# More load places for the raw queries, keys and values, and GpSimd as a third engine for SBUF passes and for the softmax division

## The chip, the cores and the metric

The kernel runs on one core of a Trainium2 chip. The metric is device time in microseconds (us), first to last instruction plus launch and end. The core has five instruction streams that run side by side and wait for each other through semaphores: TensorE (PE, matmuls; its weight loads are a row of their own, PEld), VectorE (DVE), ScalarE (ACT), GpSimd (POOL) and SyncE (SP), which here issues nearly all DMAs. Each takes its instructions strictly in the order of its own queue. GpSimd reads and writes SBUF only, not PSUM.

## The reference

Inputs are float64. Attention with 8 global keys and a local window of 96 keys, then a two-layer ELU network over the same rows:

```python
scores = 1/sqrt(D) * q @ k.T                    # B=4, H=8, S=768, D=64
keep   = (pos_k < 8) | (0 <= pos_q - pos_k < 96)
scores = where(keep, scores - slope[h] * dist, -1e9)
a      = exp(scores - max);  a = a / (sum(a) + 1e-9)
x      = (a @ v), heads side by side            # 3072 x 512
h      = x @ w_in                               # 512 -> 2048
g      = where(h > 0, h, exp(min(h, 0)) - 1)
out    = g @ w_out                              # 2048 -> 512, float32
```

## The kernel before

**Work.** The 3072 rows are 12 groups of 256 (two tiles of 128). For a group the attention of 8 heads (four head pairs) gives x, kept as a rounded half `xh` and a rest `xl`; then 16 chunks `fc` of the hidden layer follow: 12 matmuls into `h` (line 623: xh with both halves of w_in, xl with one), an ELU over ScalarE and VectorE into `e` (629 to 631), its rounded half `gh` (ScalarE, 632) and rest `gl` (VectorE or GpSimd, 633), and 6 matmuls into `o` (645). Weights come as float64 bits; `weight` (360) turns each 128x512 piece into fp32 by one ScalarE and four VectorE passes (374 may go to GpSimd), rounds it into the upper half of `w` (381) and subtracts for the lower half (393, VectorE).

**Attention.** Groups 0 to 3 use `heads32`: queries are scaled in place (420), scores, softmax, a division of `pr` by the row sum (`norm`, 497, from 533; ScalarE or VectorE), a PE transpose into `t`, a copy into `pt`, and the product with the values into `pv`. Groups 4 to 11 use `head`: the same softmax, the division (578, VectorE only), a 32x32 transpose on VectorE (584), and a trip through DRAM (`dd`) that turns the blocks into `ph`.

**Order.** Nothing is ordered by hand. Every step is an `Op` with a due time, and for each engine that may take it a cost in ns and a flag that says whether it occupies the port that the planner lets VectorE and GpSimd share. `Plan.order` (102) is a greedy list scheduler: it picks the engine and the next step by these costs, due times and free buffers ("slots"), and so fixes each engine's queue. What runs is this queue, whatever the steps really last. `SLOTS` and `EARLY` (730 to 750) say which SBUF places a class of tile may use: raw queries and values are `rqv`, raw keys `rk`. In the first groups they lie in places of weights 12 to 15 and of other tiles that are not in use yet. A load is issued on SP's queue once its place is free, and loads of weights from chunk 2 on stand behind the loads of the heads that the builder had listed by then (714).

**Start.** Until the first `h` matmul the run writes fill matmuls (`none<-fill`, 806) wherever the planner's PE would idle over 300 ns, one per 240 ns of it.

Of the kernel before, what the change touches and what calls it, by code (L numbers as in the profile page):

```python
# [12 lines left out]
ALU = mybir.AluOpType  # L13
# [3 lines left out]
P = 128  # L17
# [3 lines left out]
W = NT * P  # L21
BIG = float(2 ** 100)

HI, LO = 0, 1
# [181 lines left out]
def act(n, psum=False, extra=0.0):  # L206
    return (("ACT", (55 if psum else 97) + 0.834 * n + extra, False),)


def dve(n, fast=False, port=False):  # L210
    return (("DVE", (75 + 0.521 * n) if fast else (70 + 1.042 * n), fast or port),)


def pool(n, two=True):
    return (("POOL", (30 + 2.58 * n) if two else (50 + 1.1 * n), True),)
# [25 lines left out]
class Kernel:  # L241
# [118 lines left out]
    def weight(self, which, fc, due, after):  # L360
        nc, p, DM = self.nc, self.plan, self.DM
        tag = f"w{which}{fc}"
        bits = self.sb(tag, "bits", [P, 2 * DM], I32)
        g = self.sb("io", "g", [P, DM], I32)
        w = self.sb(tag, f"w{which}", [P, 2, DM], F32R)
        src = (self.w_in, self.w_out)[which][fc].bitcast(I32)
        words = lambda: bits.t.rearrange("p (n w) -> p n w", w=2)
        low, high = lambda: words()[:, :, 0], lambda: words()[:, :, 1]
        gf = lambda: g.t.bitcast(F32)
        p.add(sp(), lambda e: nc.sync.dma_start(bits.t, src), writes=[bits], due=due - 9000, after=after, nbytes=P * DM * 8)  # L370

        p.add((("ACT", 575.0, False),), lambda e: nc.scalar.activation(gf(), high().bitcast(F32), AF.Abs), [bits], [g], due - 6000)  # L372
        p.add(dve(DM, True) + (("POOL", 640.0, True),),
              lambda e: self.on(e).tensor_scalar(gf(), gf(), F64_MAX, F64_MIN, ALU.min, ALU.max), [g], [g], due - 5500)  # L374
        p.add(dve(DM, True), lambda e: nc.vector.tensor_scalar(g.t, g.t, 3, 0x3FFFFFFF, ALU.logical_shift_left, ALU.bitwise_and),
              [g], [g], due - 5000)
        p.add(dve(DM, port=True), lambda e: nc.vector.scalar_tensor_tensor(g.t, high(), -0x40000000, g.t, ALU.bitwise_and, ALU.bitwise_or),  # L377
              [bits, g], [g], due - 4500)
        p.add(dve(DM, port=True), lambda e: nc.vector.scalar_tensor_tensor(g.t, low(), 29, g.t, ALU.logical_shift_right, ALU.bitwise_or),
              [bits, g], [g], due - 4000)  # L380
        p.add(act(DM), lambda e: self.copy(e, w.t[:, HI], gf()), [g], [w], due - 3000)
        if (which, fc) in self.ON_PE:

            lw = self.bank("lw", "lw", [P, DM], ["h0", "h1"])

            def lower(e):
                nc.tensor.matmul(lw.t, self.ident.t, gf(), start=True, stop=False)
                nc.tensor.matmul(lw.t, self.minus1.t, w.t[:, HI], start=False, stop=True)

            p.add((("PE", 1500.0, False),), lower, [g, w], [lw], due - 2500)  # L390
            p.add(act(DM, True), lambda e: self.copy(e, w.t[:, LO], lw.t), [lw], [w], due - 2000)
        else:
            p.add(dve(DM, port=True), lambda e: self.minus(e, w.t[:, LO], gf(), w.t[:, HI]),
                  [g, w], [w], due - 2000)
        return w


    def pair(self, b, gi, hp, xh, xl, due, step, X):
        nc, p = self.nc, self.plan
# [4 lines left out]
        rows = X.get("rows")  # L404
        rep = 1 if rows else 2
        nq, nk = rep * W, rep * KW
        rqv = self.sb("rqv", "rqv", [P, nq + VC], slots=X.get("rqv"))
        rk = self.sb("rk", "rk", [P, nk], slots=X.get("rk"))
# [3 lines left out]
        q32 = lambda: rqv.t[:, :nq].rearrange("p (j w) -> p j w", j=rep)  # L412
        v32 = lambda: rqv.t[:, nq:].rearrange("p (t j d) -> p t j d", t=2 * NT, j=2)
        k32 = lambda: rk.t.rearrange("p (j w) -> p j w", j=rep)
        if rows:

            if "pr" in X:
                self.loads += loads
            sc = self.scale.t[:, hp:hp + 1]
            p.add(act(W) + dve(W, True), lambda e: self.scaled(e, q32()[:, 0], q32()[:, 0], sc), [rqv], [rqv], due - 9000)  # L420
            pv = self.bank("pv", "pv", [P, NT, P], X.get("pv"))
            for tiles in (range(NT),) if X.get("whole") else ((i,) for i in range(NT)):
                self.heads32(b, hp, t0, tiles, q32, k32, v32, rqv, rk, pv, due - 2 * step, 2 * step, X)
            pvs = lambda: pv.t.rearrange("p i w -> p (i w)")
            p.add(act(W, True) + dve(W), lambda e: self.copy(e, xh.t[:, hp], pvs()), [pv], [xh], due + 700)
            p.add(dve(W), lambda e: self.minus(e, xl.t[:, hp], pvs(), xh.t[:, hp]), [pv, xh], [xl], due + 800)
            if "pr" in X:
                self.held += [o for v in (rqv, rk) for o in v.readers]
            return
# [5 lines left out]
        for j in range(2):  # L435
            sc = self.q_scale(2 * hp + j)
# [3 lines left out]
        for j in range(2):  # L440
            sc = self.q_scale(2 * hp + j)
# [12 lines left out]
        x = self.sb("x", "x", [P, W])  # L454
        head = [slice(0, 64), slice(64, 128)]
        for j in range(2):
# [3 lines left out]
            r, o, d = head[j], head[1 - j], due + (NT * j - NT) * step  # L460
# [8 lines left out]
    def scaled(self, e, out, x, sc):  # L469
        if e == "ACT":  # L470
            self.nc.scalar.activation(out, x, AF.Copy, scale=sc)
        else:
            self.nc.vector.tensor_scalar(out, x, sc, None, ALU.mult)  # L473

# [13 lines left out]
    def inverse(self, st, due, slack=0.0):  # L488
# [5 lines left out]

        self.plan.add((("DVE", 290.0, False),), inverse, [st], [st], due, slack=slack)

    def norm(self, pr, lo, st, i, due, both):
        n = 2 * P - lo
        return self.plan.add((act(n, extra=90) if both else ()) + (("DVE", 130 + 0.53 * n, True),), lambda e: self.scaled(
            e, pr.t[:, lo:], pr.t[:, lo:], st.t[:, 2, i:i + 1]), [pr, st], [pr], due)  # L500

    def heads32(self, b, hp, t0, tiles, q32, k32, v32, rqv, rk, pv, due, step, X):
# [50 lines left out]
    def head(self, b, h, t0, j, qd, ql, ks, vd, pv, due, step):  # L553

        nc, p, slack = self.nc, self.plan, self.SLACK
        st = self.sb("st", "st", [P, 3, NT])
# [18 lines left out]
        for i, pr in enumerate(prs):  # L575
            d = base + i * step
            lo = 0 if t0 + i else P
            self.norm(pr, lo, st, i, d - 3000, False)

            def turn(e, i=i, pr=pr, lo=lo):  # L580
                nc.vector.transpose(tr.t[:, :, lo // P:, i].rearrange("p b a r -> p a b r"),  # L581
                                    pr.t[:, lo:].rearrange("p (a b r) -> p a b r", b=4, r=32))

            p.add(dve(2 * P - lo), turn, [pr], [tr], d - 2500)
        if not t0:
            p.add((("DVE", 200.0, False),), lambda e: nc.vector.memset(tr.t[:, :, 0, 0], 0.0), [], [tr], base - 2600)
        flat = lambda x: x.rearrange("p b a i r -> p (b a i r)")
# [23 lines left out]
    def moe(self, rows, xh, xl, f0, f1, dues, step, part, X, last):  # L611
# [4 lines left out]
        def up(fc, d):  # L616
            w1 = ws[0][fc]
            h = self.bank("h", "h", [P, W])
            for n in range(3):
                def mm1(e, n=n, h=h, w1=w1):  # L620
                    s, x = ((HI, xh), (LO, xh), (HI, xl))[n]
                    for cc in range(self.NCC):
                        nc.tensor.matmul(h.t, w1.t[:, s, cc * P:(cc + 1) * P], x.t[:, cc],  # L623
                                         start=n == 0 and cc == 0, stop=n == 2 and cc == self.NCC - 1)
                p.add(pe(self.NCC * W), mm1, [w1, xl if n == 2 else xh], [h], d + n)
            ex = self.sb("e", "e", [P, W])
            gh, gl = self.sb("gh", "gh", [P, W], F32R), self.sb("gl", "gl", [P, W], F32R)

            p.add(act(W, True), lambda e: nc.scalar.activation(ex.t, h.t, AF.Relu, scale=-1.0), [h], [ex], d - 8000)  # L629
            p.add(act(W), lambda e: nc.scalar.activation(ex.t, ex.t, AF.Exp, scale=-1.0), [ex], [ex], d - 8000)  # L630
            p.add(dve(W), lambda e: nc.vector.scalar_tensor_tensor(ex.t, ex.t, -1.0, h.t, ALU.add, ALU.max), [h, ex], [ex], d - 8000)  # L631
            p.add(act(W), lambda e: self.copy(e, gh.t, ex.t), [ex], [gh], d - 8000)
            p.add(dve(W, port=True) + pool(W) if X or last else (("POOL", 787.0, True),), lambda e: self.minus(e, gl.t, ex.t, gh.t), [ex, gh], [gl], d - 8000)
            G[fc] = gh, gl

# [46 lines left out]
    def build(self):  # L682
# [41 lines left out]
        for _, f in sorted(todo, key=lambda x: x[0]):  # L724
# [4 lines left out]

    LATE = 12  # L730
    ON_PE = []
    FIRST = {"rqv": ["rqv0", "w015", "w115"], "rk": ["rk0", "w014", "w114"], "pr": ["pr0", "pr1", "pr2", "w013", "w113"],
             "pt": ["pt0", "pt1", "w012", "w112"], "rows": True}
    EARLY = [dict(FIRST, rqv=FIRST["rqv"] + ["part0", "part1"], rk=FIRST["rk"] + ["qd0", "ql0"], pr=FIRST["pr"] + ["ks0"],
                  pt=FIRST["pt"] + ["vd0"], t=["t0", "h0"], s=["s0", "s1", "o0", "o1"], pv=["v0"]), dict(FIRST, whole=True), dict(FIRST, whole=True),
             {"rqv": ["rqv0", "ks0"], "rk": ["rk0", "qd0", "ql0"], "rows": True, "whole": True}, {}]

    SLACK, LATER = 600.0, 1200.0

# [286 lines left out]
```

## Time and profile before

| what | value |
|---|---|
| time, median of 3 runs (range) | 690.71 us (689.43 to 692.09) |
| the profiled execution | 689.4 us, span 687.6 us |
| PE, DVE, ACT, POOL busy | 667.9, 556.6, 498.3, 222.1 us |
| share of the span | 97%, 81%, 72%, 32% |
| HBM | 73.01 MB read, 23.07 MB written |

Busy PE is not PE at its peak: a matmul's end is modelled, so gaps shorter than its pipeline don't show, and fill matmuls count as busy. The idle time before a group of instructions and its releaser, and the table by stretches, tell more than the share of the span.

### The profile page before, as it was taken

The numbers are of one execution on the slowest core, as the hardware profiler recorded it, in microseconds if no ns is written. First come the engines' busy times: TensorE is split into PE (matmuls) and PEld (weight loads), VectorE is DVE, ScalarE is ACT, GpSimd is POOL, SyncE is SP. The second block draws the span as 40 slices with busy tenths as digits, with TensorE's granted clock in tenths as the row PEclk, the third lists the DMA queues.
The fourth block names the chain that finished last, engine by engine and source line by source line (L and its number), as shares of the span: only waits on it lengthen the run. The fifth ranks groups of instructions, "written<-read, shape, count | busy, mean of one in ns | idle before, by whom it ended". The sixth has DMA issues, their size and how long they took to land.

```text
span 687.6 us, 13611 instructions
## 1 busy us (share of the span) xinstructions
PE 667.9 (97%) x4461; PEld 590.4 (86%) x4461; DVE 556.6 (81%) x1647; ACT 498.3 (72%) x1400; POOL 222.1 (32%) x277
## 2 busy tenths in 40 slices
PE   9989999999999998999999999999999999999996
PEld 6768788888888987989989989989999989889895
DVE  6999999997649999978978998987888997983322
ACT  6998897885657777867867777867967867775443
POOL 1110222120014453452454463353364445233000
PEclk9999999999999999999999999999999999999999
DMA  8543980010136547455453553643652653520000
GB/s 319 194 116 114 412 340 24 1 48 1 55 122 218 163 147 210 139 171 161 154 182 111 183 153 124 209 157 103 229 164 88 228 158 107 178 93 1 32 1 33
DMA packets 65259, 97.01 MB, mean 141 GB/s; under 512 B 4640, under 2 KB 39712, under 8 KB 65184
## 3 DMA queue, kind: packets, MB, share of 16 engines
q1 hardware_dynamic: 64896, 95.96, 42.2%
q8 instruction: 36, 0.59, 0.4%
q14 instruction: 39, 0.32, 0.1%
q10 hardware_dynamic: 288, 0.13, 0.1%
HBM read 73.01 MB, written 23.07 MB: 140 GB/s over the span
## 4 chain that ended last, share of the span: by engine, by line
PE 60%; DVE 21%; ACT 7%; issue 6%; DMA 5%; POOL 1%; SPq 0%; DVEq 0%; POOLq 0%; ACTq 0%
PE h L623 26%; PE o L645 26%; DVE pr L473 3%; PE pv L604 3%; DVE tr L581 3%; ACT pr L485 2%; DVE pr L483 2%; PE s L570 2%; DVE e L631 2%; DVE x L464 2%; DVE ph L300 2%; DMA bits<-in_w_out_dram 1%; DVE ks L300 1%; DVE g L377 1%; DMA ph<-dd 1%
## 5 line engine op out<-in xcount | busy, mean ns | idle before, releaser
L623 PEld LDWEIGHTS h<-xh,w 128*128 128x128 f32 x1536 | 230.7, 189 | 30.3 <-ACT xh L292 1.4
L645 PE MATMUL o<-w,gh 128*128 128x512 f32 x768 | 242.7, 399 | 4.8 <-ACT gh L292 2.5
L623 PE MATMUL h<-xh,w 128*128 128x256 f32 x1536 | 243.4, 282 | 1.8 <-ACT xh L292 1.2
L300 POOL TENSOR_TENSOR gl<-e,gh 128x256 fp32r<-128x256 f32 x135 | 109.6, 812 | 287.2 <-ACT gh L292 251.6
L645 PEld LDWEIGHTS o<-w,gh 128*128 128x128 f32 x768 | 124.4, 188 | 20.4 <-ACT gh L292 8.8
L631 DVE SCALAR_TENSOR_TENSOR e<-e,h 128x256 f32<-128x256 f32 x192 | 79.7, 415 | 61.8 <-ACT e L630 58.3
L645 PE MATMUL o<-w,gl 128*128 128x512 f32 x384 | 128.1, 396 | 0.0
L623 PE MATMUL h<-xl,w 128*128 128x256 f32 x768 | 121.7, 280 | 0.0
L292 ACT CAST gh<-e 128x256 fp32r<-128x256 f32 x192 | 77.5, 404 | 59.5 <-DVE e L631 58.2
L629 ACT ACTIVATE e<-h 128x256 f32<-128x256 f32 x192 | 72.7, 379 | 58.8 <-PE h L623 54.9
L485 ACT ACTIVATE pr<-pr,nmax 128x256 f32<-128x256 f32 (+1 forms) x192 | 93.5, 487 | 21.5 <-DVE nmax L483 20.3
L623 PEld LDWEIGHTS h<-xl,w 128*128 128x128 f32 x768 | 104.0, 188 | 0.3 <-issue 0.2
L630 ACT ACTIVATE e<-e 128x256 f32<-128x256 f32 x192 | 79.8, 416 | 3.8
L483 DVE CUSTOM_DVE_ANT_0 pr<-s,tab 128x256 f32<-128x256 f32 (+1 forms) x192 | 72.5, 389 | 10.9 <-PE s L570 8.9
L473 DVE TENSOR_SCALAR pr<-pr,st 128x256 f32<-128x256 f32 (+1 forms) x159 | 65.6, 436 | 0.6
L645 PEld LDWEIGHTS o<-w,gl 128*128 128x128 f32 x384 | 62.3, 189 | 2.9 <-issue 0.5
L464 DVE TENSOR_TENSOR x<-pv,x 64x256 f32<-64x256 f32 x128 | 53.1, 415 | 9.2 <-ACT x L292 6.7
L581 DVE STREAM_TRANSPOSE tr<-pr 128x256 f32<-128x256 f32 (+1 forms) x128 | 52.6, 417 | 0.4
L374 POOL TENSOR_SCALAR g<-g 128x512 f32<-128x512 f32 x24 | 22.8, 955 | 91.6 <-ACT g L372 86.9
L300 DVE TENSOR_TENSOR ph<-ph 128x512 fp32r<-128x512 f32 x62 | 46.1, 744 | 2.3 <-ACT ph L292 2.0
L300 POOL TENSOR_TENSOR vd<-rqv,vd 128x512 fp32r<-128x512 f32 (+1 forms) x32 | 40.2, 1255 | 1.7
L292 ACT CAST ph<-ph 128x512 fp32r<-128x512 f32 x64 | 39.1, 611 | 1.8 <-DMA ph<-dd 1.7
(93 smaller groups left out, 844.6 us busy)
## 6 DMA issues: line engine op xcount, KB each, us to landing
rqv<-in_qkv_dram SPq DMA_DIRECT2D x32, 512.0 KB, 4.1
dd<-tr SPq DMA_DIRECT2D x64, 256.0 KB, 2.5
ph<-dd SPq DMA_DIRECT2D x64, 256.0 KB, 3.0
rk<-in_qkv_dram SPq DMA_DIRECT2D x32, 400.0 KB, 4.0
bits<-in_w_in_dram SPq DMA_DIRECT2D x16, 512.0 KB, 8.9
bits<-in_w_out_dram SPq DMA_DIRECT2D x16, 512.0 KB, 9.9
rqv<-in_qkv_dram SPq DMA_DIRECT2D x16, 384.0 KB, 3.7
out_dram<-ob SPq DMA_DIRECT2D x23, 256.0 KB, 3.7
```

Source lines behind the costliest of these rows:

```text
L292: self.nc.scalar.copy(out, x)
L300: self.on(e).tensor_tensor(out, x, y, ALU.subtract)
L464: p.add(dve(W), lambda e, r=r, s=s, xt=xt, pv=pv: nc.vector.tensor_tensor(xt(), pv.t[r, :, s], xt(), ALU.add), [pv, x], [x], d + 600 + s)
L473: self.nc.vector.tensor_scalar(out, x, sc, None, ALU.mult)
L483: p.add((("DVE", 158 + 1.042 * n, False),), lambda e: nc.vector.tensor_tensor_reduce(pr.t[:, lo:], s.t[:, m, lo:], tab, -(2.0 ** -(h + 1)) ...
L485: p.add(act(n, extra=200), lambda e: nc.scalar.activation(pr.t[:, lo:], pr.t[:, lo:], AF.Exp, bias=nm, scale=-1.0, accum_out=st.t[:, 0, i: ...
L581: nc.vector.transpose(tr.t[:, :, lo // P:, i].rearrange("p b a r -> p a b r"), pr.t[:, lo:].rearrange("p (a b r) -> p a b r", b=4, r=32))
L623: nc.tensor.matmul(h.t, w1.t[:, s, cc * P:(cc + 1) * P], x.t[:, cc], start=n == 0 and cc == 0, stop=n == 2 and cc == self.NCC - 1)
L629: p.add(act(W, True), lambda e: nc.scalar.activation(ex.t, h.t, AF.Relu, scale=-1.0), [h], [ex], d - 8000)
L630: p.add(act(W), lambda e: nc.scalar.activation(ex.t, ex.t, AF.Exp, scale=-1.0), [ex], [ex], d - 8000)
L631: p.add(dve(W), lambda e: nc.vector.scalar_tensor_tensor(ex.t, ex.t, -1.0, h.t, ALU.add, ALU.max), [h, ex], [ex], d - 8000)
L645: nc.tensor.matmul(acc[i].t, g.t[:, i * P:(i + 1) * P], w2.t[:, s], start=fc == f0 and n == 0 and s == HI, stop=fc == f1 - 1 and n == 1)
```

## The change

Three more places for `rqv` in groups 0 to 3 (the `ph` buffers, free until group 4) and two more for `rk` in groups 1 and 2 are listed in `FIRST` and `EARLY`; the lower weight half goes to GpSimd alone, and GpSimd may take the upper half, the scaling of the queries, the division of the first groups, and `gh` of the first three groups. The division of groups 4 to 11 goes to GpSimd alone. The planner's cost of the 32x32 transpose rises and gets a slack.

```diff
-        p.add(act(DM), lambda e: self.copy(e, w.t[:, HI], gf()), [g], [w], due - 3000)
+        p.add(act(DM) + pool(DM, False), lambda e: self.copy(e, w.t[:, HI], gf()), [g], [w], due - 3000)
...
-            p.add(dve(DM, port=True), lambda e: self.minus(e, w.t[:, LO], gf(), w.t[:, HI]),
+            p.add(pool(DM), lambda e: self.minus(e, w.t[:, LO], gf(), w.t[:, HI]),
...
-            p.add(act(W) + dve(W, True), lambda e: self.scaled(e, q32()[:, 0], q32()[:, 0], sc), [rqv], [rqv], due - 9000)
+            p.add(act(W) + dve(W, True) + (("POOL", 60 + 1.1 * W, True),), lambda e: self.scaled(e, q32()[:, 0], q32()[:, 0], sc), [rqv], [rqv], due - 9000)
...
+        elif e == "POOL":
+            self.nc.gpsimd.tensor_scalar(out, x, sc, 1.0, ALU.mult, ALU.mult)
...
+    def divide(self, pr, lo, st, i, due):
+        n = 2 * P - lo
+        self.plan.add((("POOL", 60 + 1.1 * n, True),), lambda e: self.nc.gpsimd.tensor_scalar(
+            pr.t[:, lo:], pr.t[:, lo:], st.t[:, 2, i:i + 1], 1.0, ALU.mult, ALU.mult), [pr, st], [pr], due)
...
-        return self.plan.add((act(n, extra=90) if both else ()) + (("DVE", 130 + 0.53 * n, True),), lambda e: self.scaled(
+        return self.plan.add((act(n, extra=90) if both else ()) + (("DVE", 130 + 0.53 * n, True), ("POOL", 60 + 1.1 * n, True)), lambda e: self.scaled(
...
-            self.norm(pr, lo, st, i, d - 3000, False)
+            self.divide(pr, lo, st, i, d - 3000)
...
-            p.add(dve(2 * P - lo), turn, [pr], [tr], d - 2500)
+            p.add((("DVE", 150 + 1.042 * (2 * P - lo), False),), turn, [pr], [tr], d - 2500, slack=300.0)
...
-            p.add(act(W), lambda e: self.copy(e, gh.t, ex.t), [ex], [gh], d - 8000)
+            p.add(act(W) + (pool(W, False) if X else ()), lambda e: self.copy(e, gh.t, ex.t), [ex], [gh], d - 8000)
...
-    FIRST = {"rqv": ["rqv0", "w015", "w115"], "rk": ["rk0", "w014", "w114"], "pr": ["pr0", "pr1", "pr2", "w013", "w113"],
+    FIRST = {"rqv": ["rqv0", "w015", "w115", "ph0", "ph1", "ph2"], "rk": ["rk0", "w014", "w114", "qd0", "ql0"], "pr": ["pr0", "pr1", "pr2", "w013", "w113"],
...
-             {"rqv": ["rqv0", "ks0"], "rk": ["rk0", "qd0", "ql0"], "rows": True, "whole": True}, {}]
+             {"rqv": ["rqv0", "ks0", "ph0", "ph1", "ph2"], "rk": ["rk0", "qd0", "ql0"], "rows": True, "whole": True}, {}]
```

Over the whole program the division of `pr` moves from 159 VectorE and 33 ScalarE instructions to 18, 25 and 149 on GpSimd; the lower weight half from 32 on VectorE to 32 on GpSimd; the scaling of queries from 7 VectorE and 9 ScalarE to 1, 8 and 7 on GpSimd; 12 `gh` and 6 upper weight halves go from ScalarE to GpSimd; of the 32 clamps of `weight` (374) GpSimd had 24 and has 26.

SP's queue before, from the load of the fifth pair's keys on (`rqv` and `rk` are loads of a head pair, `bits` a weight; a tile's number grows with its place in the plan):

```order
L411 DMA rk_159<-in_qkv_dram 128x400
L370 DMA bits_162<-in_w_in_dram 128x1024
L370 DMA bits_164<-in_w_out_dram 128x1024
L370 DMA bits_166<-in_w_out_dram 128x1024
L370 DMA bits_194<-in_w_in_dram 128x1024
L370 DMA bits_205<-in_w_in_dram 128x1024
L370 DMA bits_213<-in_w_out_dram 128x1024
L370 DMA bits_221<-in_w_out_dram 128x1024
L411 DMA rk_283<-in_qkv_dram 128x400
L411 DMA rk_356<-in_qkv_dram 128x400
```

The same place now:

```order
L411 DMA rk_159<-in_qkv_dram 128x400
L410 DMA rqv_161<-in_qkv_dram 128x768
L410 DMA rqv_163<-in_qkv_dram 128x768
L370 DMA bits_165<-in_w_in_dram 128x1024
L410 DMA rqv_173<-in_qkv_dram 128x768
L370 DMA bits_179<-in_w_out_dram 128x1024
L370 DMA bits_183<-in_w_out_dram 128x1024
L411 DMA rk_191<-in_qkv_dram 128x400
L370 DMA bits_202<-in_w_in_dram 128x1024
L370 DMA bits_213<-in_w_in_dram 128x1024
```

Three loads of queries and values of the second group have moved ahead of the first weights. Further on in the same queue, the last loads of the third group and the weights of chunk 4 behind them stood so before:

```order
L410 DMA rqv_787<-in_qkv_dram 128x768
L410 DMA rqv_824<-in_qkv_dram 128x768
L410 DMA rqv_998<-in_qkv_dram 128x768
L410 DMA rqv_1006<-in_qkv_dram 128x768
L370 DMA bits_1045<-in_w_in_dram 128x1024
L370 DMA bits_1051<-in_w_in_dram 128x1024
```

and now:

```order
L410 DMA rqv_598<-in_qkv_dram 128x768
L411 DMA rk_660<-in_qkv_dram 128x400
L410 DMA rqv_685<-in_qkv_dram 128x768
L410 DMA rqv_690<-in_qkv_dram 128x768
L370 DMA bits_729<-in_w_in_dram 128x1024
L370 DMA bits_735<-in_w_in_dram 128x1024
```

The same loads and weights have moved from tile number 1045 to 729 of the plan. On PE, the last rows ahead of the first `h` matmul of group 0 (`pv` a product with values, `t` transposes, `s` scores) were before:

```order
L522 MATMUL pv_364<-pt_391,rqv_147 64x128 x4
L806 MATMUL none<-fill 128x512 x6
L522 MATMUL pv_444<-pt_407,rqv_153 64x128 x2
L540 MATMUL t_447<-ident,pr_360 128x128 x2
L540 MATMUL t_447<-ident,pr_389 128x128 x2
L806 MATMUL none<-fill 128x512 x5
L516 MATMUL s_470<-rk_283,rqv_426 128x256
L516 MATMUL s_471<-rk_283,rqv_426 128x256
```

and now:

```order
L523 MATMUL s_407<-rk_159,rqv_157 128x256
L523 MATMUL s_408<-rk_159,rqv_157 128x256
L813 MATMUL none<-fill 128x512
L529 MATMUL pv_433<-pt_395,rqv_153 64x128 x2
L813 MATMUL none<-fill 128x512 x3
L547 MATMUL t_450<-ident,pr_378 128x128 x2
L547 MATMUL t_450<-ident,pr_393 128x128 x2
L813 MATMUL none<-fill 128x512 x3
L523 MATMUL s_468<-rk_191,rqv_161 128x256
```

Seven fills stand where eleven stood; over the whole start it is 33 instead of 43, with the same attention work ahead of the first `h`. In a late group, VectorE's rows between a row sum's inverse (`st`) and the transposes were before:

```order
L493 RECIPROCAL st_8590<-st_8590 128x2
L631 SCALAR_TENSOR_TENSOR e_8621<-e_8621,h_8568 128x256
L473 TENSOR_SCALAR pr_8566<-pr_8566,st_8590 128x256
L473 TENSOR_SCALAR pr_8603<-pr_8603,st_8590 128x256
L581 STREAM_TRANSPOSE tr_8650<-pr_8566 128x2x4x32
```

Now GpSimd's queue has the two divisions of that head, between the rest `gl` of one chunk and of the next:

```order
L300 TENSOR_TENSOR gl_8592<-e_8542,gh_8582 128x256
L501 TENSOR_SCALAR pr_8556<-pr_8556,st_8571 128x256
L501 TENSOR_SCALAR pr_8588<-pr_8588,st_8571 128x256
L300 TENSOR_TENSOR gl_8651<-e_8615,gh_8639 128x256
```

The transposes on VectorE stay behind them across engines, with other VectorE work in between.

## Rows read from the trace of the kernel before

**Rows 1.** Busy time by stretches of the span: the stretch, its length, then busy us and (x instructions) of PE, PEld, DVE, ACT and POOL, the granted PE clock, the DMA share and GB/s.

```profile
0.00:30.00 30.00, 28.50 (x170) 19.42 (x171) 24.05 (x116) 22.72 (x73) 4.84 (x23) 1.00 0.72 275
30.00:80.00 50.00, 45.81 (x374) 36.82 (x373) 46.23 (x165) 44.39 (x140) 6.20 (x9) 1.00 0.53 182
80.00:200.00 120.00, 119.75 (x802) 104.69 (x801) 101.18 (x249) 85.28 (x226) 21.36 (x20) 1.00 0.26 97
200.00:620.00 420.00, 411.96 (x2730) 374.06 (x2729) 365.30 (x1066) 316.99 (x894) 183.92 (x217) 1.00 0.50 159
620.00:687.60 67.60, 61.88 (x394) 55.42 (x392) 19.79 (x53) 28.90 (x72) 5.78 (x9) 0.99 0.05 17
```

**Rows 2.** What PE waited for in the whole span: us in total, times, longest us.

```profile
PE o L645 <- ACT gh L292: 2.5, 5, 1.0
PE t L540 <- DVE pt L294: 1.6, 1, 1.6
...
PE s L516 <- ACT rqv L471: 1.3, 1, 1.3
PE h L623 <- ACT xh L292: 1.2, 1, 1.2
```

**Rows 3.** PE's instructions in order of time in the start: start us, us, what, how many.

```profile
8.32 0.50 PE L806 MATMUL none<-fill 128*128 128x512 f32 x1
...
23.85 1.65 PE L806 MATMUL none<-fill 128*128 128x512 f32 x6
...
29.61 1.68 PE L623 MATMUL h<-xh,w 128*128 128x256 f32 x12
...
37.66 0.66 PE L540 MATMUL t<-ident,pr 128*128 128x128 f32 x4 [1.55 <-DVE pt L294]
39.57 1.14 PE L516 MATMUL s<-rk,rqv 64*128 64x256 f32 x8 [1.25 <-ACT rqv L471]
```

**Rows 4.** The fill matmuls as one group in the first 40 us: count, busy us, mean ns, idle before.

```profile
L806 PE MATMUL none<-fill 128*128 128x512 f32 x43 | 15.6, 492 | 1.4 <-POOL fill L324 1.4
```

**Rows 5.** SP's queue in order of time: start us, us from first to last issue, what.

```profile
35.60 0.33 SPq L410 DMA_DIRECT2D rqv<-in_qkv_dram  x1
...
41.77 0.33 SPq L410 DMA_DIRECT2D rqv<-in_qkv_dram  x1
...
48.91 15.62 SPq L410 DMA_DIRECT2D rqv<-in_qkv_dram  x4
64.59 0.90 SPq L370 DMA_DIRECT2D bits<-in_w_in_dram  x2
```

**Rows 6.** Pieces of the chain that ended last, between 30 and 80 us: start us, us, what.

```profile
35.60 3.39 DMA rqv<-in_qkv_dram
...
41.77 3.59 DMA rqv<-in_qkv_dram
...
65.53 9.16 DMA bits<-in_w_out_dram
```

**Rows 7.** VectorE groups of the whole span by shape: count, busy us, mean ns, idle before.

```profile
L473 DVE TENSOR_SCALAR pr<-pr,st 128x256 f32<-128x256 f32 x133 | 57.9, 455 | 0.4
...
L492 DVE TENSOR_SCALAR st<-st 128x2 f32<-128x2 f32 x96 | 24.0, 250 | 6.5 <-ACT pr L485 6.0
...
L300 DVE TENSOR_TENSOR w<-g,w 128x512 fp32r<-128x512 f32 x32 | 21.8, 682 | 0.2
...
L473 DVE TENSOR_SCALAR pr<-pr,st 128x128 f32<-128x128 f32 x26 | 8.6, 339 | 0.1
```

**Rows 8.** The same groups between 30 and 80 us alone.

```profile
L300 DVE TENSOR_TENSOR w<-g,w 128x512 fp32r<-128x512 f32 x8 | 5.5, 682 | 0.1
L473 DVE TENSOR_SCALAR pr<-pr,st 128x256 f32<-128x256 f32 x15 | 5.1, 357 | 0.0
...
L492 DVE TENSOR_SCALAR st<-st 128x2 f32<-128x2 f32 x14 | 2.3, 164 | 0.4 <-ACT pr L485 0.3
...
L473 DVE TENSOR_SCALAR rqv<-rqv,scale 128x256 f32<-128x256 f32 x5 | 1.7, 348 | 0.4 <-DMA rqv<-in_qkv_dram 0.4
```

**Rows 9.** GpSimd groups by shape: first the whole span, then the first 30 us, then 30 to 200 us, then 200 to 620 us.

```profile
L300 POOL TENSOR_TENSOR vd<-rqv,vd 128x512 fp32r<-128x512 f32 x24 | 32.0, 1333 | 1.1
...
L294 POOL CAST vd<-rqv 128x384 fp32r<-128x384 f32 x8 | 4.1, 512 | 2.7 <-PE pv L604 2.6
...
L374 POOL TENSOR_SCALAR g<-g 128x512 f32<-128x512 f32 x4 | 2.4, 626 | 13.0 <-ACT g L372 13.0
...
L374 POOL TENSOR_SCALAR g<-g 128x512 f32<-128x512 f32 x20 | 20.4, 1020 | 78.6 <-ACT g L372 73.9 <-DVE w L300 4.7
...
L300 POOL TENSOR_TENSOR gl<-e,gh 128x256 fp32r<-128x256 f32 x122 | 99.9, 819 | 203.4 <-ACT gh L292 179.3 <-PE o L645 10.1 <-PE h L623 9.3
```

More of the change, by code (lines that the diff above doesn't have):

```diff
@@ L731 @@
     ON_PE = []
-    FIRST = {"rqv": ["rqv0", "w015", "w115"], "rk": ["rk0", "w014", "w114"], "pr": ["pr0", "pr1", "pr2", "w013", "w113"],
+    FIRST = {"rqv": ["rqv0", "w015", "w115", "ph0", "ph1", "ph2"], "rk": ["rk0", "w014", "w114", "qd0", "ql0"], "pr": ["pr0", "pr1", "pr2", "w013", "w113"],
              "pt": ["pt0", "pt1", "w012", "w112"], "rows": True}
-    EARLY = [dict(FIRST, rqv=FIRST["rqv"] + ["part0", "part1"], rk=FIRST["rk"] + ["qd0", "ql0"], pr=FIRST["pr"] + ["ks0"],
+    EARLY = [dict(FIRST, rqv=FIRST["rqv"] + ["part0", "part1"], pr=FIRST["pr"] + ["ks0"],
                   pt=FIRST["pt"] + ["vd0"], t=["t0", "h0"], s=["s0", "s1", "o0", "o1"], pv=["v0"]), dict(FIRST, whole=True), dict(FIRST, whole=True),
-             {"rqv": ["rqv0", "ks0"], "rk": ["rk0", "qd0", "ql0"], "rows": True, "whole": True}, {}]
+             {"rqv": ["rqv0", "ks0", "ph0", "ph1", "ph2"], "rk": ["rk0", "qd0", "ql0"], "rows": True, "whole": True}, {}]
     SLACK, LATER = 600.0, 1200.0
```

## The prediction

> **What bounds the kernel now.** I read the table by stretches first, then what PE waited for, then PE's and SP's rows in order of time in the start, then the groups by shape. The reader is to see in the table [rows 1] that PE is the bound nearly everywhere: from 80 to 200 us it is idle for 120.00 - 119.75 = 0.25 us, from 200 to 620 us for 420 - 411.96 = 8.0 us. The granted clock is 1.00 in both, the upper level of 2.4 GHz, so it has no part in this. The change adds or takes no matmul of the computation; all it can do is shorten or lengthen the time in which PE has nothing useful to do. That time is 4.2 us from 30 to 80 us (50 - 45.81), 8.0 us later, the 43 fills of the start [rows 4], and little else: the idle time of the last stretch is mostly the end, after PE's last matmul. So some 22 us is the most that can be won, and the question is how much of each piece goes.
>
> In the early stretch the other engines are nearly full: VectorE 46.23 and ScalarE 44.39 of 50 us, GpSimd 6.20. And the chain that ended last runs there through loads [rows 6]: 3.39 and 3.59 us for two loads of queries and values, 9.16 us for a weight. SP's rows [rows 5] show why they are late: the loads of the second and third group go out one by one, six us apart, since three places make each wait for an earlier pair to be used up; four more take until 64.5, and only then, at 64.59, does the weight of chunk 4 leave. SP is idle in between.
>
> **The change part by part, start to 30 us.** Ahead of the first `h`, at 29.61 us [rows 3], stand 33 fills in place of 43, with the same attention work: by the planner's costs PE waits 10 x 240 ns less. A single fill shows 0.50 us and six in a row 1.65, so one costs (1.65 - 0.50) / 5 = 0.23 us; by mean busy time [rows 4] it would be 0.49. I take 10 x 0.23 = 2.3 us won; the ends are 4.9 won, and 1 us lost if GpSimd's passes come late and PE stands idle where the fills were. What pays for it is that some scalings and divisions of the first pairs leave VectorE and ScalarE for GpSimd.
>
> **30 to 80 us.** With six places instead of three, the loads at 35.60 and 41.77 [rows 5] go out while the first pairs are worked on. The two stalls behind them, 1.55 and 1.25 us on PE [rows 2, 3], lose their cause: scaled queries and copies that came late because a load did or VectorE was full. VectorE is also relieved: 8 lower weight halves (5.5 us), most of 15 divisions (5.1) and of 5 scalings (1.7) [rows 8], about 10 of its 46 us. GpSimd takes 8 x 1.33 us for the halves [rows 9] and some 16 divisions and scalings. A division of 128x256 on GpSimd is not in the trace; the nearest rows are its 128x512 one-input pass with 626 ns, half of which is 0.31 us, and a 128x384 copy with 512 ns [rows 9]. I take 0.37 us, nearer the first since it is the same operation. That makes 6.2 + 10.6 + 5.9 = 22.7 of 50 us on GpSimd: room enough. What is late next are the transposes' copies on two engines that are still 70% to 90% full, so of 4.2 us idle I take 3.0 as won; the ends are all 4.2, and 1 us lost.
>
> The weights: the last loads of the third group need a place that a pair three pairs earlier gives up, so chunk 4 leaves about when four pairs of the second group are done, some 15 to 20 us before 64.59. This takes the 9.16 us off the chain, but PE waited only briefly for it, and that is within the 3.0.
>
> **80 to 200 us.** 24 lower halves (24 x 0.682 = 16.4 us [rows 7]) go from VectorE to GpSimd, where they last 24 x 1.33 = 32 us. PE has 0.25 us idle, so a relief of VectorE is worth nothing here: 0, with a loss of up to 12 us if GpSimd can't keep up (first rival).
>
> **200 to 620 us.** Eight groups with 16 divisions each: 112 of 128x256 and 16 of 128x128 leave VectorE, 112 x 0.455 + 16 x 0.339 = 56 us [rows 7], and GpSimd gets 128 x 0.37 = 47 us (40 to 66 by the two ends). VectorE falls from 365 of 420 us (87%) to 309 (74%), GpSimd rises from 184 (44%) to 231 (55%) [rows 1]. The hop to another engine and back lies between the inverse and the transposes; other VectorE steps are put there in the new order. PE's 8.0 us idle here is scattered over short waits for `gh` and `xh` [rows 2], both made of ScalarE and VectorE steps that queue behind attention work. A quarter of VectorE's queue is gone in front of them, and the planner now counts the transpose near what it lasts. I take 3.0 of the 8.0 us as won; ends 8.0 won and 12 lost (second rival).
>
> VectorE's and GpSimd's passes hold each other up, and the trace has the size: the inverse's first step, 128x2, lasts 164 ns where GpSimd is 12% busy [rows 8, 1] and 250 in the mean [rows 7]; GpSimd's clamp lasts 626 ns in the first 30 us and 1020 from 30 to 200 us, where VectorE is full [rows 9]. With GpSimd's share up by a quarter, 96 inverses lose perhaps a quarter of 86 ns more, 2 us in all on an engine that gives up 56, so I book nothing.
> The Trainium skill ("SBUF — State Buffer", Who interferes with whom) makes this a lock: a VectorE operation in a two-port mode or with two SBUF inputs, or a GpSimd operation, holds the shared port pair for the whole instruction, and the other blocks. The stretched rows agree with it; by it the move wins less than its 56 us of VectorE, because a division on GpSimd holds the pair too. It also speaks against the lower halves, as "GPSIMD Engine Reference" (Engine selection) does, which puts two-input passes at about twice VectorE's time; the trace agrees with 1333 against 682 ns.
>
> **Sum.** -2.3 - 3.0 + 0 - 3.0 = -8.3 us on the profiled execution's 689.4: 681.1. Its time lies 1.3 us under the median of the runs, so against 690.71 I forecast 682.4 us (-1.2%).
>
> **The rivals.** First, on the other side: GpSimd becomes the bound of the weight stage. A chunk is used by three groups, 3 x 18 matmuls; at 61.88 us for 394 instructions [rows 1] that is 54 x 0.157 = 8.5 us a chunk. GpSimd's share of it: two lower halves, two clamps (26 of 32 clamps are its), up to two `gl` and a cast or two. Undisturbed: 2 x 1.33 + 2 x 0.63 + 2 x 0.82 + 0.7 = 6.3 us. Stretched like the clamp (1020 / 626 = 1.63): 2.2 x 2 + 1.0 x 2 + 1.6 + 1.2 = 9.2, beyond 8.5: it decides from a stretch of about 1.5 on all of its passes. Then each of 12 chunks comes about 1 us late, +12 us, less 5.3 won before: 697. For it: the clamp's rows. Against: VectorE's own port work falls by a third there, GpSimd had only 21 us of 120 to do [rows 1], and weights leave earlier and have a lead.
>
> Second: the division holds up the late groups. GpSimd takes its queue in order; `gl` waits there 203.4 / 122 = 1.7 us each for `gh` [rows 9], and a division behind it waits too, then the transposes on VectorE, the trip through DRAM, and at a group's end PE for `xh`. If all eight group ends pay 1.7 us, it is +13, less the 1.2 that one shows already [rows 2] and less 5.3: +6.7 us, 697. Against: only one such wait is in the trace at all, so the chains have a lead.
>
> Third: little changes. The fills' 2.3 us come, but stalls between 30 and 80 us only change their releaser, from loads to full VectorE and ScalarE, and the short waits later stay, being the greedy order's own: 688.4. For it: 92% and 89% busy there. Nor need the change do what it says about division: where the planner finds VectorE cheaper, `norm` stays; but 149 of 192 are on GpSimd.
>
> **How the numbers follow.** The forecast has 62% (its own range 675 to 687), little change 20%, each of the two slower cases 9%. About 0.5% (3.5 us) is what a measurement of this kernel can tell from no change: from 687.3 to 694.2. Faster: the 62 and 2 of the third case, 64%; no difference: the rest of the third and 2 of the slower ones, 20%; slower 16%. The range: the won ends add up to 4.9 + 4.2 + 8.0 = 17 us, 674; upward it takes in the third case and half-sized losses, to 694, and leaves most of the two slower cases out.
>
> **What would show it.** In the new profile: the first `h` near 27 us; loads of queries no longer six us apart, chunk 4's weight leaving before 52 us; PE idle under 2 us from 30 to 80 us; VectorE near 74% and GpSimd near 55% from 200 to 620 us with PE idle about 5 us there; a division on GpSimd of about 0.37 us, 0.6 at most. Wrong would be: PE idle of several us between 80 and 200 us with `w` or `gl` of GpSimd as releaser (first rival), or waits for `xh` at every group's end (second).

## The result, and the profile after

The changed kernel takes 674.22 us (673.97 to 675.37 over 6 runs), the kernel before 691.4 us on the same chip; the ratio is 0.9757 with a 95% interval from 0.9733 to 0.9780. That is 16.8 us less (0.0243 x 691.4), where 8.3 were forecast. The time lies 0.2 us above the low end of the range.

The table by stretches of the changed kernel, with the columns of [rows 1]:

```profile
0.00:30.00 30.00, 28.28 (x172) 19.15 (x173) 23.75 (x112) 22.30 (x76) 13.32 (x38) 1.00 0.90 343
30.00:80.00 50.00, 47.42 (x370) 37.07 (x369) 48.44 (x150) 44.32 (x134) 25.99 (x34) 1.00 0.72 263
80.00:200.00 120.00, 120.00 (x810) 106.00 (x810) 99.58 (x240) 80.75 (x211) 55.96 (x59) 1.00 0.15 53
200.00:620.00 420.00, 419.99 (x2814) 385.13 (x2813) 328.01 (x943) 322.64 (x902) 250.75 (x347) 1.00 0.50 157
```

Read the instruction counts beside the busy time. From 200 to 620 us PE is idle for 0.01 us instead of 8.0, but it issues 2814 instructions instead of 2730. An instruction of the tail takes 61.88 / 394 = 0.157 us [rows 1], so 84 more (59 of them `h`, 25 `o`) are 13.2 us of work: 5 us more than the idle time shows. From 80 to 200 us 8 more (1.3 us). Up to 80 us there are 172 + 370 - 33 fills = 509 against 170 + 374 - 43 = 501, another 1.3 us, though matmuls of several kinds are mixed there. Together 15.7 us, about the gain (the two profiled executions lie 15.2 us apart), and more than four fifths of it is in the late groups.

What PE still waited for, in the whole span:

```profile
PE s L523 <- DVE nmax L485: 1.4, 2, 1.2
PE none L813 <- POOL fill L324: 1.4, 1, 1.4
PE h L630 <- DVE e L638: 0.6, 1, 0.6
PE o L652 <- POOL w L300: 0.4, 1, 0.4
```

Four rows are left, and `xh` and `gh` of [rows 2] are gone from them. GpSimd's new passes, and the first step of the inverse on VectorE:

```profile
L501 POOL TENSOR_SCALAR pr<-pr,st 128x256 f32<-128x256 f32 x112 | 60.8, 552 | 30.2 <-DVE st L495 17.4 <-ACT gh L292 6.3 <-ACT xh L292 2.9
L300 POOL TENSOR_TENSOR w<-g,w 128x512 fp32r<-128x512 f32 x32 | 43.5, 1366 | 25.6 <-ACT w L292 25.3
...
L501 POOL TENSOR_SCALAR pr<-pr,st 128x128 f32<-128x128 f32 x16 | 7.4, 461 | 6.6 <-ACT x L292 3.6 <-DVE st L495 3.0
```

```profile
L494 DVE TENSOR_SCALAR st<-st 128x2 f32<-128x2 f32 x96 | 32.6, 339 | 7.9 <-ACT pr L487 7.1
```

A division on GpSimd lasts 0.55 us, not 0.37, and the inverse 339 ns instead of 250.

SP's queue in the start, against [rows 5]:

```profile
34.03 0.33 SPq L410 DMA_DIRECT2D rqv<-in_qkv_dram  x1
37.70 0.33 SPq L411 DMA_DIRECT2D rk<-in_qkv_dram  x1
39.36 0.80 SPq L410 DMA_DIRECT2D rqv<-in_qkv_dram  x2
40.21 0.90 SPq L370 DMA_DIRECT2D bits<-in_w_in_dram  x2
```

Chunk 4's weights leave at 40.21 us instead of 64.59. The first `h` starts at 27.90 us instead of 29.61.

### The profile page after: what moved, and what is told of

It is laid out like the page before. It is cut to its first block, busy times and chain, and to the rows that moved or that the text cites. A ratio compares the mean times of both kernels' runs of the same rounds, so it can differ in the third digit from the quotient of the medians.

```text
span 672.4 us, 13656 instructions
## 1 busy us (share of the span) xinstructions
PE 662.2 (98%) x4451; PEld 588.7 (88%) x4451; DVE 513.6 (76%) x1475; ACT 490.9 (73%) x1371; POOL 346.8 (52%) x478
## 4 chain that ended last, share of the span: by engine, by line
PE 90%; DVE 6%; ACT 2%; DMA 1%; issue 0%; ACTq 0%
PE o L652 39%; PE h L630 39%; PE s L577 4%; PE pv L611 4%; PE s L523 1%; PE pv L529 1%; PE t L547 1%; DVE st L494 1%; DVE pr L485 1%; ACT pr L487 1%; DMA n_raw<-in_n_dram 1%; DVE g L377 1%; DVE g L379 1%; ACT pt L292 1%; DVE pr L475 0%
## 5 line engine op out<-in xcount | busy, mean ns | idle before, releaser
L300 POOL TENSOR_TENSOR gl<-e,gh 128x256 fp32r<-128x256 f32 x130 | 105.7, 813 | 119.3 <-ACT gh L292 94.6
L292 ACT CAST gh<-e 128x256 fp32r<-128x256 f32 x180 | 72.5, 403 | 52.0 <-DVE e L638 50.1
L487 ACT ACTIVATE pr<-pr,nmax 128x256 f32<-128x256 f32 (+1 forms) x192 | 93.6, 488 | 13.3 <-DVE nmax L485 12.1
L501 POOL TENSOR_SCALAR pr<-pr,st 128x256 f32<-128x256 f32 (+1 forms) x128 | 67.8, 541 | 36.8 <-DVE st L495 20.4
L300 POOL TENSOR_TENSOR w<-g,w 128x512 fp32r<-128x512 f32 x32 | 43.5, 1366 | 25.6 <-ACT w L292 25.3
L300 DVE TENSOR_TENSOR ph<-ph 128x512 fp32r<-128x512 f32 x64 | 50.8, 793 | 2.8 <-ACT ph L292 2.3
L300 POOL TENSOR_TENSOR vd<-rqv,vd 128x512 fp32r<-128x512 f32 (+1 forms) x32 | 42.0, 1312 | 1.9
L300 DVE TENSOR_TENSOR gl<-e,gh 128x256 fp32r<-128x256 f32 x62 | 32.9, 533 | 12.1 <-ACT gh L292 10.0
```

Of the source, the lines that this page charges most:

```text
L292: self.nc.scalar.copy(out, x)
L300: self.on(e).tensor_tensor(out, x, y, ALU.subtract)
L487: p.add(act(n, extra=200), lambda e: nc.scalar.activation(pr.t[:, lo:], pr.t[:, lo:], AF.Exp, bias=nm, scale=-1.0, accum_out=st.t[:, 0, i: ...
L501: self.plan.add((("POOL", 60 + 1.1 * n, True),), lambda e: self.nc.gpsimd.tensor_scalar(pr.t[:, lo:], pr.t[:, lo:], st.t[:, 2, i:i + 1], 1 ...
```

## The experiments

The trace alone does not say which edit won what. The theories: R, VectorE is relieved of the late divisions; O, later sharpened to T, the plan is truer because VectorE's steps are no longer counted too short; E, split into P (places, earlier loads) and Q (GpSimd's early passes), the gain comes from the start. All ratios are to the kernel before on the same chip.

| run | ratio, 95% interval | median us | PE instr. 200 to 610 us | VectorE busy there, us |
|---|---|---|---|---|
| before | 1 | 690 to 691 | 2665 | 357.7 |
| late_both | 0.9842 (0.9807 to 0.9878) | 679.56 | 2731 | 323.5 |
| divide_only | 0.9873 (0.9841 to 0.9906) | 681.04 | 2729 | 327.1 |
| cost_only | 0.9964 (0.9943 to 0.9984) | 687.85 | 2674 | 355.8 |
| one_column | 0.9848 (0.9818 to 0.9879) | 679.43 | 2727 | 336.4 |
| true_cost | 0.9928 (0.9902 to 0.9953) | 686.50 | 2699 | 354.1 |
| ballast | 1.0176 (1.0145 to 1.0208) | 703.70 | 2554 | 339.2 |
| ballast_known | 0.9877 (0.9848 to 0.9906) | 682.14 | 2697 | 351.3 |
| changed | 0.9757 (0.9733 to 0.9780) | 674.22 | 2747 | 323.9 |

**The late groups: parts alone.**

```diff
+            self.divide(pr, lo, st, i, d - 3000)                                # late_both, divide_only
+            p.add((("DVE", 150 + 1.042 * (2 * P - lo), False),), turn, ..., slack=300.0)  # late_both, cost_only
```

> The kernel before with the two edits of the late groups alone: the division of groups 4 to 11 on GpSimd, and the transpose's new cost and slack. Table of the new profile: 84 more PE instructions between 200 and 620 us, 8 more in each of the two earlier stretches. Theory R (the relief of VectorE in the late groups carries the gain) and theory O (the truer cost of the transpose carries it) both expect 11 to 14 us less than before, PE idle under 1 us from 200 to 620 us. Theory E (earlier loads and the early passes on GpSimd shift everything behind them) expects at most 4 us less.

> The kernel before with the division of groups 4 to 11 on GpSimd alone, the transpose's cost as before. R: 9 to 13 us less than before, PE idle under 2 us from 200 to 620 us (8.0 before). O: 0 to 3 us less, or slower, since GpSimd's division shows 0.55 us where the planner counts 0.34 and the transpose is still counted 80 ns short. E: within 2 us of before.

> The kernel before with the transpose's new cost and slack alone, the division still on VectorE. O: 8 to 13 us less than before. R: within 3 us of before, since VectorE stays 87% busy from 200 to 620 us. E: within 2 us.

The two late edits give 0.0158 x 690 = 10.9 us, the division alone 8.8, the transpose's cost alone 2.5. E is out as the only cause: it allowed the late edits 4 us at most. O is out as it stood: it expected 8 to 13 us of the transpose's cost alone. R fits in the main: 10.9 and 8.8 lie just under its low ends of 11 and 9, and late_both issues 67 more instructions than before from 200 to 620 us (2797 against 2730), not 84, and none more before that.

**The same order with a shorter division.**

```diff
-            self.norm(pr, lo, st, i, d - 3000, False)
+            self.one(pr, lo, st, i, d - 3000)   # same cost in the plan, x = pr.t[:, lo:lo + 1]
```

> The kernel before with every engine's order kept, and the division of groups 4 to 11 cut to one column of 128x256 or 128x128; the other columns stay undivided. VectorE loses about 128 x 0.3 us and nothing else changes, no step moves, nothing goes to GpSimd. R: most of the late gain, 7 to 12 us less than before, PE idle under 2 us from 200 to 620 us. O: within 2 us of before, since the order is the same. E: within 2 us.

The run leaves all columns of `pr` but one undivided, so it serves for its time alone. It gives 10.5 us without a step moved and without GpSimd:

```profile
200.00:610.00 410.00, 407.82 (x2727) 373.77 (x2726) 336.39 (x1066) 316.82 (x892) 183.70 (x217) 1.00 0.51 163
```

```profile
L473 DVE TENSOR_SCALAR pr<-pr,st 128x1 f32<-128x1 f32 x128 | 22.6, 201 | 0.5
```

So O in its first form, a better order, is not needed for the gain. But the run can't tell R from T: the division fell from 474 ns to 201, under the 266 that the plan counts, so it is both less work and a plan no longer too short.

**Which of the two.** VectorE's division lasts 474 ns from 200 to 620 us in the kernel before and the transpose 433, where its plan counts 266 and 337: 304 ns too little per tile.

```profile
L473 DVE TENSOR_SCALAR pr<-pr,st 128x256 f32<-128x256 f32 x112 | 50.9, 474 | 0.4
L581 DVE STREAM_TRANSPOSE tr<-pr 128x256 f32<-128x256 f32 x112 | 47.9, 433 | 0.4
```

```diff
+        self.plan.add((("DVE", 204 + 1.055 * n, True),), ...            # true_cost: division stays on VectorE
+                nc.vector.tensor_scalar(self.load[:, lo:], self.load[:, lo:], 1.0, None, ALU.mult)  # ballast, in turn
-            p.add((("DVE", 150 + 1.042 * (2 * P - lo), False),), turn, ...
+            p.add((("DVE", 590 + 1.042 * (2 * P - lo), False),), turn, ...   # ballast_known
```

> The kernel before with the division of groups 4 to 11 still on VectorE, but counted by the planner at what it lasts there (474 ns for 256 columns, 339 for 128, instead of 266 and 198), and the transpose's new cost and slack. No work changes its engine. Theory T (the late gain is a plan that no longer undercounts VectorE: 266 + 337 ns planned per tile against 474 + 433): 6 to 11 us less than before, 680 to 684 us, PE idle under 3 us from 200 to 620 us. R (VectorE's relief): within 4 us of before, as the transpose's cost alone gave 2.5 us.

> The changed kernel, every engine's order kept, with a 128x256 (or 128x128) one-input pass over a tile of its own on VectorE ahead of each of the 128 transposes: some 128 x 0.35 us put back on VectorE. R (VectorE's relief is the late gain): most of it is lost again, 682 to 687 us, PE idle 4 us or more from 200 to 620 us. Theory S (what counts is that the division no longer stands in VectorE's queue between inverse and transpose, that is the order): 674 to 677 us.

> The ballast kernel (703.7 us) with the 440 ns of the added pass counted in the planner's cost of the transpose (590 instead of 150 ns of fixed part). VectorE does the same extra work. T: most of the ballast's 29 us comes back, 675 to 684 us. R: 690 us or more, VectorE being as full as before the change.

Ballast put 112 x 0.438 us and 16 shorter passes back on VectorE behind the plan's back, and cost 29.5 us over the changed kernel, far more than R said (682 to 687 us); theory S, for which the order alone counts (674 to 677), is out:

```profile
200.00:610.00 410.00, 394.51 (x2554) 355.09 (x2553) 339.18 (x990) 297.58 (x835) 225.99 (x320) 0.98 0.49 155
```

```profile
L590 DVE TENSOR_SCALAR ballast<-ballast 128x256 f32<-128x256 f32 x112 | 49.1, 438 | 0.3
```

VectorE is less full here than before the change (339 of 410 us against 358), and yet PE has lost 193 instructions against the changed kernel's 2747. Some 7 us of the loss is PE's clock: the mean granted over the profiled execution is 0.989, against 0.999 in the changed kernel (0.010 x 703.7). With the same work counted in the plan, 21.6 of the 29.5 us come back (20.7 of 28.9 by the ratios, since the runs were on two chips), with VectorE busier:

```profile
200.00:610.00 410.00, 405.18 (x2697) 369.23 (x2696) 351.29 (x1038) 312.36 (x876) 252.99 (x344) 1.00 0.50 160
```

How full VectorE is does not by itself set the time; whether the order allowed for the work does, first of all. R's 690 or more is refuted. Yet T alone is not enough either: true_cost gives 5.0 us, with an interval of 3.2 to 6.8 that only just reaches T's 6 to 11 and stays under the 8.4 to 13.3 of late_both, and ballast_known stays 7.9 us above the changed kernel. The late 11 us are thus some 5 of truer counting, had without moving any work, and some 6 that came only with the work moved. The split is of two greedy orders and holds within their scatter of a few us.

**The early part.** Beside the late edits' 1.6% the whole change has another 0.85%.

```diff
+    FIRST = {"rqv": [..., "ph0", "ph1", "ph2"], "rk": [..., "qd0", "ql0"], ...   # places; late_places with the late edits
+            p.add(pool(DM), lambda e: self.minus(e, w.t[:, LO], ...              # early_pool, with the other first-group edits
```

after_old_places is the changed kernel with the old `FIRST` and `EARLY`.

> The kernel before with the new places for queries, values and keys alone (FIRST and EARLY); no work changes its engine. Theory P (the earlier loads carry the early gain of the change, 5 to 6 us beside the late groups'): 3 to 6 us less than before; chunk 4's weight leaves near 45 us instead of 64.59. Theory Q (GpSimd's passes carry it, the loads were hidden behind VectorE and ScalarE, which stay full): within 2 us of before, although the weight leaves as early.

> The kernel before with GpSimd's passes of the first groups alone: lower weight half on GpSimd, upper half, scaling of queries, division of groups 0 to 3 and gh of groups 0 to 2 as a third choice. The places and the late groups stay as before. Q: 3 to 6 us less than before. P: within 2 us of before, the loads still six us apart and chunk 4's weight near 60 us.

> The changed kernel with the places of before. P: 4 to 6 us more than the changed kernel's 674.2, near the 679.6 of the two late edits alone. Q: at most 1 us more, 673 to 675. If both are needed together: 2 to 4 us more.

> The kernel before with the two late edits and the new places, without GpSimd's passes of the first groups. If the places need GpSimd's passes (the earlier weights only move work onto a full VectorE): 678 to 682 us, as the late edits alone (679.6). If the places carry the early gain by themselves once the late groups follow: 672 to 676 us.

| run | ratio, 95% interval | median us | PE instr. 80 to 200 us | chunk 4 leaves at us |
|---|---|---|---|---|
| before | 1 | 690.5 | 802 | 64.59 |
| places | 1.000 (0.9984 to 1.0016) | 691.00 | 801 | 40.32 |
| early_pool | 1.0051 (1.0036 to 1.0066) | 694.19 | 754 | 62.60 |
| after_old_places | 0.9885 (0.9864 to 0.9906) | 683.16 | 760 | 63.77 |
| late_places | 0.9859 (0.9834 to 0.9884) | 680.65 | 794 | 40.52 |
| changed | 0.9757 (0.9733 to 0.9780) | 674.22 | 810 | 40.21 |

Both P and Q fall: places alone win nothing, GpSimd's passes alone cost 3.5 us, and on top of the late edits each still wins nothing or costs (0.9859 and 0.9885 against 0.9842, with intervals that overlap). Together they win 5.9 us there (0.0085 x 691), so each is worth more once the other is in: 8.8 us for the places (0.9885 - 0.9757), 7.0 us for the passes (0.9859 - 0.9757). late_places came where it was expected if the places need the passes; but P, Q and the case that both are needed all gave the changed kernel with the old places a loss of at most 6 us, and it lost 8.8. The pair without the late edits was not run. Not all of the 5.9 us is early: from 200 to 610 us late_places and the changed kernel both issue 2747 instructions, late_both 2731. What late_places lacks it has lost before 200 us.

Why GpSimd's passes alone lose is in early_pool's chain between 84 and 108 us:

```profile
85.02 8.03 DMA bits<-in_w_in_dram
...
96.56 1.43 DVE gl L300
98.00 1.17 DVE st L494
...
104.34 1.67 DVE g L379
106.01 0.34 DVE e L633
...
106.39 1.74 PE h L625 x12
```

The chain comes out of a weight that lands at 93.05. It left at 85.02, and the weights from chunk 4 on, of which it is one, start to leave at 62.60 only, behind loads that wait for places. VectorE takes its queue in order, so the conversion of that weight stands before the steps that PE needs. And beside it GpSimd works on two lower halves:

```profile
96.25 2.88 POOL L300 TENSOR_TENSOR w<-g,w 128x512 fp32r<-128x512 f32 x2 [4.55 <-ACT w L292]
104.19 1.27 POOL L300 TENSOR_TENSOR w<-g,w 128x512 fp32r<-128x512 f32 x1 [5.07 <-DVE st L494]
```

In these 2.88 us VectorE's `gl` and the inverse last 1.50 and 1.24 us, against 0.43 and 0.16 a few us later. The last conversion pass ahead of the `e` that PE waits for lasts 1.75 us beside the other row, against 0.68 just before:

```profile
96.50 1.50 DVE L300 TENSOR_TENSOR gl<-e,gh 128x256 fp32r<-128x256 f32 x1
97.92 1.24 DVE L494 TENSOR_SCALAR st<-st 128x2 f32<-128x2 f32 x1
...
101.50 0.43 DVE L300 TENSOR_TENSOR gl<-e,gh 128x256 fp32r<-128x256 f32 x1 [0.42 <-ACT gh L292]
...
102.78 0.68 DVE L379 SCALAR_TENSOR_TENSOR g<-bits,g 128x512 int32<-128x512 int32 x1
...
103.98 0.16 DVE L494 TENSOR_SCALAR st<-st 128x2 f32<-128x2 f32 x1
...
104.26 1.75 DVE L379 SCALAR_TENSOR_TENSOR g<-bits,g 128x512 int32<-128x512 int32 x1
```

PE then stands still for 2.95 us, the longest part of the 5.1 us that it is idle from 80 to 200 us; the rest was not followed:

```profile
106.39 1.19 PE L625 MATMUL h<-xh,w 128*128 128x256 f32 x8 [2.95 <-DVE e L633]
```

Late weights alone are not the cause: the kernel before has them 2 us later still (64.59), and PE is idle for 0.25 us from 80 to 200 us. What early_pool adds is GpSimd's passes and the stretching by them, which shows in VectorE's means from 80 to 200 us, first before, then in early_pool:

```profile
L300 DVE TENSOR_TENSOR gl<-e,gh 128x256 fp32r<-128x256 f32 x33 | 14.4, 437 | 3.1 <-ACT gh L292 3.0
```

```profile
L300 DVE TENSOR_TENSOR gl<-e,gh 128x256 fp32r<-128x256 f32 x32 | 20.3, 635 | 7.4 <-ACT gh L292 4.8 <-POOL gh L294 2.5
```

With weights 22 to 24 us earlier this wait is gone: from 80 to 200 us PE issues 810 instructions, although `gl` still lasts 598 ns there. The other half, why the places alone win nothing, is shown only as far as this: in places VectorE is busy 104.3 of 120 us from 80 to 200 (101.2 before, 99.6 in the changed kernel), PE is idle 2.9 us there, and between 30 and 80 us it issues 329 instructions at a granted clock of 0.93. The profiled execution of places took 694.27 us, 3.3 more than the run's median, and lost some 3.5 us of full speed to the clock there (0.07 x 50), so these rows show more of a loss than most executions had. My reading, which no run tests: earlier weights bring their four or five passes to engines that have no room yet.

**GpSimd's division at its true price.**

```diff
-        self.plan.add((("POOL", 60 + 1.1 * n, True),), ...
+        self.plan.add((("POOL", 270 + 1.1 * n, True),), ...
```

> The changed kernel with GpSimd's division of groups 4 to 11 counted at what it lasts (552 ns for 256 columns instead of 342). T, taken to GpSimd: 1 to 3 us less than the changed kernel's 674.2. R: within 1 us of it, since PE has under 4 us left to win from 200 us on and GpSimd is 60% busy; a new greedy order may also cost up to 3 us.

674.47 us, ratio 0.9760 (0.9737 to 0.9782): no difference. T, taken to GpSimd, expected 1 to 3 us and is missed; R's 1 us holds. The plan counts GpSimd's division 210 ns too short, but PE has nothing left to win from 200 us on, and GpSimd is busy 60% of that stretch. That an undercount costs only where an engine has little room is a reading that no run tests. No run beat the changed kernel.

## Why the prediction was right, and which sizes were off

**Right**: the direction, the bound (PE, with other engines' lateness as the only thing to win), chunk 4's weight (forecast before 52 us, 40.21), the first `h` (near 27, 27.90), GpSimd's fuller queue without any wait of PE at the groups' ends. The time is in the range, at its edge, and just outside the 675 to 687 that the forecast case gave as its own. That it is inside is in part luck: the late term came 5.2 us beyond its own best end (13.2 against 8.0), and the two stretches up to 80 us 4.0 us short of what was forecast.

**Signs that missed.** PE is idle for 2.6 us from 30 to 80 us, not under 2, and GpSimd is 60% busy from 200 to 620 us, not 55%. The loads of queries still leave five to six us apart in the start (27.63, 34.03, 39.36); what moved chunk 4 is that three of them left at 8 to 11 us already.

**200 to 620 us, the term that was mis-sized.** "I take 3.0 of the 8.0 us as won": it won 13.2 by instructions. Two steps failed. The ceiling of 8.0 was the idle time that the page shows; gaps shorter than a matmul's modelled pipeline don't show in it, and PE's rate held 5 us more. And a half or less of it was taken, because the waits were put down to the greedy order's scatter; one_column, with the order unchanged, won 10.5 us by shorter work on VectorE, so most of the waits were not the order's own but VectorE running behind its plan, which counts it 304 ns a tile too short; that counting right is part of the cure, ballast_known and true_cost show. The prediction mentions the truer count of the transpose but not the division's, which was in the rows: 455 ns against a cost of 266 in the code.

**Start and 30 to 80 us.** 5.3 us were forecast, about 1.3 came. The fills' 2.3 is confirmed in kind (the first `h` 1.7 us earlier), and the 3.0 of the two stalls is not: they went, but VectorE stayed full (48.4 of 50 us, 46.2 before), and waits of 1.2 and 0.6 us for its steps took their place. In this stretch the third rival was right.

**80 to 200 us.** 0 was forecast, 1.3 us came. The first rival's loss is real, 48 instructions or 7.5 us in early_pool (3.5 us in its time, since PE was 13 instructions ahead at 80 us and won a few later), but by another step than it named: not GpSimd's own rate (the lower half lasts 1.35 us there, barely stretched, and GpSimd is busy 53.5 of 120 us) but VectorE's passes, stretched beside GpSimd while late weights stand in VectorE's queue. What decided against it was the lead that the places give, which the prediction names under "Against" and gives no size. The rival's threshold was also worked out too high: 8.5 / 6.3 is a stretch of 1.35, not 1.5.

**Sizes.** The division on GpSimd, 0.55 us, is beyond the upper end of 0.51 that the sum used, though within the 0.6 named as the most. VectorE from 200 to 620 us fell to 78%, not 74%: the 2 us of mutual stretching were too few. The inverse alone went from 250 to 339 ns, `ph` from 744 to 793 and `gl` from 431 to 533. The second rival did not come: no wait for `xh` is left.

## What to carry to other kernels

Where a planner fixes in-order queues, compare its cost of each step with what the step lasts: 0.44 us per tile that the plan did not know of cost 29.5 us here, and the same work, known, 7.9. Measure a bound engine's slack by instructions per stretch, not by idle time alone. Two edits that are worth nothing or less when tried one by one can be worth close to a percent together, when one supplies the lead that the other uses up.

## What the runs showed of the hardware

VectorE and GpSimd hold each other up by whole instructions: beside two GpSimd passes of 1.4 us, a VectorE step on 128x2 elements lasted 1.24 us instead of 0.16, about the length of one GpSimd pass. This is what the Trainium skill ("SBUF — State Buffer", Who interferes with whom) says of the shared port pair, and these rows agree. The added ballast pass, 128x256 in and out of SBUF, shows 438 ns in the mean, where VectorE's division of that shape shows 357 with GpSimd 12% busy [rows 8, 1].

A stop of PE can cost more than its own length. In early_pool, after the 2.95 us in which PE had nothing to do, the granted clock went from 1.00 (2.4 GHz) to the lower level of 1.2 GHz:

```profile
104.00:107.00 3.00, 0.60 (x5) 0.61 (x6) 2.96 (x9) 1.97 (x7) 2.29 (x2) 1.00 0.00 0
107.00:108.00 1.00, 1.00 (x11) 1.00 (x10) 1.00 (x5) 1.00 (x4) 0.31 (x1) 0.90 0.08 16
108.00:110.00 2.00, 2.00 (x6) 1.58 (x6) 1.24 (x3) 2.00 (x8) 1.93 (x2) 0.50 0.00 0
110.00:112.00 2.00, 2.00 (x10) 1.70 (x8) 1.14 (x3) 0.91 (x3) 0.93 (x1) 0.70 0.00 0
```

From 107 to 112 us the clock's share was 0.90, 0.50 and 0.70, so 0.1 + 1.0 + 0.6 = 1.7 us of full speed were lost on top. The stretch of the changed kernel that answers to it, 80 to 200 us, shows 1.00.
